# Loading a first job in one transfer, forming a decay in two parts, and placing idle transposes: a fused attention and MoE kernel

## The chip, the cores and the metric

The kernel runs on one core of one Trainium2 chip. The metric is device time in microseconds (us) of one execution. The core has a matrix engine (TensorE, PE in the profile; its weight loads are PEld), VectorE (DVE), ScalarE (ACT), GpSimd (POOL), and SyncE (SP), which here does nothing but issue DMA transfers; ScalarE can issue transfers too. Sixteen DMA engines carry the transfers of the core.

## The reference, cut to what matters

Three stages run one after the other on 4 x 576 = 2304 tokens:

```python
scores = q @ k.T / sqrt(64)                    # 4 batches x 8 heads, 576 x 576, causal
cum    = cumsum(max(s, 0))                     # one decay row of 576 per head
scores = where(causal, -1e9, scores + minimum(-(cum[q] - cum[k]), 0))
x = softmax(scores) @ v                        # -> 2304 x 512
x = (ms * relu(x @ w_in)**2 + mb) @ w_out      # 512 -> 2048 -> 512
x = maximum(x @ w1, x @ w2, x @ w3, 0) @ w_fin # 512 -> 768 -> 512
```

The weights arrive as 64-bit numbers. The result must have the accuracy of fp32, so that a product of the MoE stages is made of three matmuls on rounded parts (hi x hi, hi x lo, lo x hi), and every weight is first converted into two such parts on chip.

## The kernel before, in words

Attention is cut into jobs of one pair of heads each. The first jobs (kind A) cover the first 320 of 576 positions of a pair, the next ones (B) the rest, later ones (W) a whole pair. Query positions are taken in chunks (the first has 64 rows, the others 128); chunk `i` sees the first `W[i]` = 64, 192, 320, 448, 576 keys. For each chunk ("unit") of a job and both heads of the pair the kernel does: scores in PSUM (`qk`, L542: raw q by raw k, and L544: the decay of the chunk `dd` by a one-hot `oh` that picks the head), mask and row minimum on DVE (`least`, L563), exponential and row sum on ACT (`expo`, L569), transposes on PE (`turn_p`, L612) and a copy of them (L245 on ACT, L249 on DVE), product with v (L631). The reciprocal of the row sums (`rr`, L582) is turned (L586), split (`rt`, L594) and spread (L602), and multiplied into `x` (L639). The first MoE product (L256 to L258) begins between the jobs, and fills PE from then on.

The decay is formed once for all heads: `s` (32 heads x 576) is loaded four times, into the four groups of 32 partitions, so that both heads of a pair and both of their parts have it in place (four transfers at L342, two of them issued by ACT). L352 takes the maximum with zero, L353 makes the running sum over all 576 columns, and `difference(i)` (L358) makes the part of chunk `i` in `df`. ACT rounds `df` into `dh` (L361 for chunks 0 to 2 at once, L519 for chunks 3 and 4), and DVE makes from both the operand `dd` (L362, L523). L445 makes `dm`, a copy of the running sum that jobs of kind W load later.

A weight piece is one transfer from SP (L281) into `wg`, `stage` or `wst` and eight steps: L286 on ACT, then L289, L291, L295, L297 on DVE, a rounding (L245 on ACT or L249 on DVE), and L252 and L301 on DVE or POOL. While attention starts, these conversions are most of what DVE does.

The order on each engine is made when the program is built: a list scheduler (`Plan`) takes the steps with estimated costs, priorities, needs and buffers, and writes each engine's instructions in the order that it finds. An engine executes its list strictly in this order. `WARM` idle transposes of the identity (`warm`, L510) open PE's list. `keep` makes `KEEP` more of them in a step of lowest priority, `KEEPS` times, wherever the plan sees a hole on PE before the first MoE product; with `KEEPS` = 0 there are none. `COLD` is the planned time up to which the scheduler reckons a PE step at double cost. SP's list starts with its share of `s`, q of jobs 0 and 1 (L476, two transfers a job, one for each head), a weight piece, v, k of jobs 0 and 1 (L476), and further weight pieces.

Of the kernel before, what the change touches and what calls it, by code (L numbers as in the profile page):

```python
# [8 lines left out]
F32 = mybir.dt.float32  # L9
# [17 lines left out]
COLD = 8  # L27
DM_AT = 47.138
D_AT = -2.0
WARM = 40  # L30
KEEP = 4
KEEPS = 0
# [171 lines left out]
def fused_kernel(ctx, tc, q, k, v, s, w_in, w_out, ms, mb, w1, w2, w3, w_fin, out,  # L204
# [65 lines left out]
    def weight_steps(piece, stage_tile):  # L270
# [10 lines left out]
        nc.sync.dma_start(st.bitcast(I64), src)  # L281
# [59 lines left out]
    for g in range(4):  # L341
        (nc.sync if g < 2 else nc.scalar).dma_start(s0[g * NH:(g + 1) * NH], s.rearrange("b h s -> (b h) s"))  # L342
# [12 lines left out]
    df = atp.tile([P, OFF[-1] + W[-1]], F32, name="df", tag="p2")  # L355
    def difference(i):
# [3 lines left out]
    def split_d(a, b):  # L360
        nc.scalar.activation(dh[:, :b - a].bitcast(F32R), df[:, a:b], AF.Copy)  # L361
        nc.vector.scalar_tensor_tensor(dd[:, a:b], dh[:, :b - a], lower, df[:, a:b], op0=ALU.mult, op1=ALU.add)  # L362

    for i in range(3):
        difference(i)
    split_d(0, OFF[3])


# [316 lines left out]
    def add(key, engine, cost, prio, needs, f, *args, att=False, delay=None, **k):  # L685
# [4 lines left out]
        if engine == "SP":  # L690
            plan.add(("issue", *key), {"SP": 0.475 * cost[0] + 0.17 * (cost[0] // 3)}, prio, needs, f, *args, delay=0.65, **k)
            plan.add(key, {"DMA": cost[1] * P * 4 / 360e3}, prio, [("issue", *key)], lambda: None, delay=0.95 + (delay or 0))
            return
# [9 lines left out]
    for e, cost in (("DVE", 7.7), ("ACT", 6.8), ("Pool", 5.0)):  # L703
        add(("pre", e), e, cost, -1e9, [], lambda: None)
    add(("warm",), "PE", 0.213 * WARM / 2, -1e9, [], warm, take=[("sm", [("warm",)])])
    for i in range(3, NC):
        add(("df", i), "DVE", dve_fast(W[i]), -2.0, [("pre", "DVE")], difference, i, att=True)
        add(("dh", i), "ACT", act(W[i]), D_AT + i, [("df", i), ("dd", i - 1)], hi_d, i, att=True)
        add(("dd", i), "DVE", dve(W[i]), D_AT + i, [("dh", i)], lo_d, i, att=True)
    add(("pp",), "Pool", 1.2, 4.0, [("pre", "Pool")], rest_p, att=True)  # L710
    for x, e in enumerate(("ACT", "DVE", "DVE", "DVE")):
        add(("dm", x), e, act(S) if e == "ACT" else dve(S), DM_AT + x, [("pre", "DVE")] + [("dm", y) for y in range(x)], decays, x, att=True)
# [3 lines left out]
    for x in range(KEEPS):  # L716
        add(("keep", x), "PE", 0.109 * KEEP, 1e8, [("keep", x - 1)] if x else [("turn_p", 0, 1, 1)], keep, x, take=[] if x else [("mm", [("keep", KEEPS - 1)])])
# [3 lines left out]
    for job in jobs:  # L721
# [18 lines left out]
        if pairs:  # L740
            for key, when, m in (("q", Q_LOAD, job.q1 - job.q0), ("k", K_LOAD, job.keys)):
                add((key, n), "SP", (2, m), t0 + when, [] if key == "q" else [("q", n)], load_qk, job, key, take=[("raw", [("qk", n, u) for u in units])] if key == "q" else [], **a)
            add(("oh", n), "Pool", 0.3, t0 + TURN, [("qk", n - 2, u) for u in range(6)], one_hot, job, **a)
        else:
            for j in range(2):
                th = t0 + j * period / 2
                add(("q", n, j), "SP", (2, 2 * S), th + Q_LOAD, [], load_both, job, j, take=[("raw", [("rest", n, j, z) for z in range(PARTS)] + [("again", n, j)])], **a)
# [7 lines left out]
        for x, u in enumerate(units):  # L755
            i, k0, k1, c0, c1 = UNITS[u]
            if pairs:
# [3 lines left out]
                add(("qk", n, u), "PE", 5 * (k1 - k0) / 2400 + 0.25, at[u, 0], ready + [("dd", i) if i > 2 else ("pre", "DVE")] + [("after", z) for z in same] + order, qk, job, u,  # L761
# [65 lines left out]
    def convert(name, z, piece, stage_tile, prios, needs, ring_st, ring_a, **k):  # L827

        state = []

        def step(on=None):
            if not state:
                state.append(side_steps(piece) if name == "s" else weight_steps(piece(), stage_tile))
# [8 lines left out]
        parts = (("SP", (1, 2 * n), (), [(ring_st, back)]), ("ACT", act(n), (0,), [(ring_a, back)] if ring_a else []),  # L842
# [702 lines left out]
_INS = ['q', 'k', 'v', 's', 'moe_w_in', 'moe_w_out', 'moe_s', 'moe_b', 'moe2_w1', 'moe2_w2', 'moe2_w3', 'moe2_w_out']  # L1545
# [3 lines left out]
def _lay_out(name, a):  # L1549

    import numpy as _np
    if name in ("q", "k", "v"):
        b, h, n, d = a.shape
        if name == "v":
            a = a.reshape(b, h // 2, 2, n, d).transpose(0, 1, 3, 2, 4).reshape(b * h // 2, n, 2 * d)
        else:
            a = a.transpose(0, 1, 3, 2).reshape(b * h // 2, 2, d, n)
            a = _np.concatenate([a, a], axis=2)
# [26 lines left out]
```

## Time and profile before

| | us |
|---|---|
| median of 3 runs | 887.21 |
| lowest and highest run | 885.99, 888.48 |
| span of the profiled execution | 887.0 |
| PE busy in it | 868.2 (98%) |
| DVE busy in it | 646.5 (73%) |
| ACT busy in it | 484.7 (55%) |
| POOL busy in it | 329.1 (37%) |

The span runs from the first to the last instruction of one profiled execution. Only its span was kept, no time of its own; it lies inside the three runs' interval, 0.2 us under their median. The shares are means over the whole span: an engine with a small share can still be the one that a stage waits for, so the stretch that a change touches has to be read by itself.

### The profile page before, as it was taken

The numbers are of one execution on the slowest core, as the hardware profiler recorded it, in microseconds if no ns is written. First come the engines' busy times: TensorE is split into PE (matmuls) and PEld (weight loads), VectorE is DVE, ScalarE is ACT, GpSimd is POOL, SyncE is SP. The second block draws the span as 40 slices with busy tenths as digits, with TensorE's granted clock in tenths as the row PEclk, the third lists the DMA queues.
The fourth block names the chain that finished last, engine by engine and source line by source line (L and its number), as shares of the span: only waits on it lengthen the run. The fifth ranks groups of instructions, "written<-read, shape, count | busy, mean of one in ns | idle before, by whom it ended". The sixth has DMA issues, their size and how long they took to land.

```text
span 887.0 us, 16239 instructions
## 1 busy us (share of the span) xinstructions
PE 868.2 (98%) x5374; PEld 784.5 (88%) x5374; DVE 646.5 (73%) x1587; ACT 484.7 (55%) x1211; POOL 329.1 (37%) x361
## 2 busy tenths in 40 slices
PE   7999999999999999999999999999999999999998
PEld 6668888888888989999988888888999899989996
DVE  7999588888986888794859799744666566656650
ACT  6878999999955454453546364451225322532221
POOL 3344567566631332342324151320224322522220
PEclk9999999999999999999999999999999999999999
DMA  6654555655552466464747748449999156815501
GB/s 204 186 157 149 172 167 170 214 161 176 174 172 73 124 189 215 144 244 132 256 122 273 274 151 310 151 149 251 300 303 273 72 166 176 229 72 166 166 25 71
DMA packets 155268, 159.16 MB, mean 179 GB/s; under 512 B 10545, under 2 KB 121393, under 8 KB 155185
## 3 DMA queue, kind: packets, MB, share of 16 engines
q1 hardware_dynamic: 155088, 157.98, 57.5%
q8 instruction: 43, 0.70, 0.3%
q14 instruction: 41, 0.33, 0.1%
q10 hardware_dynamic: 96, 0.15, 0.0%
HBM read 113.72 MB, written 44.37 MB: 178 GB/s over the span
## 4 chain that ended last, share of the span: by engine, by line
PE 75%; DVE 10%; ACT 6%; DMA 5%; issue 2%; SPq 1%; POOL 0%; DVEq 0%; ACTq 0%; POOLq 0%
PE mm L256 22%; PE mm L257 22%; PE mm L258 22%; PE pt L612 3%; PE px L631 3%; PE ps L552 3%; DMA wst<-in_moe_w_out_dram 3%; ACT pp L569 2%; ACT pt L245 1%; DVE pp L563 1%; DMA x_d<-x 1%; DVE g L1037 1%; PE pr L602 1%; DMA stage<-in_moe_w_in_dram 1%; ACT set L486 1%
## 5 line engine op out<-in xcount | busy, mean ns | idle before, releaser
L252 POOL TENSOR_TENSOR gbl<-g,gbh 128x512 fp32r<-128x512 f32 (+1 forms) x50 | 64.8, 1297 | 124.5 <-ACT gbh L245 123.9
L1041 ACT ACTIVATE g<-g 128x512 f32<-128x512 f32 (+3 forms) x98 | 50.6, 516 | 79.8 <-DVE g L1037 79.1
L569 ACT ACTIVATE pp<-pp,mn 64x64 f32<-64x64 f32 (+4 forms) x160 | 88.7, 558 | 3.1 <-DVE mn L563 3.1
L252 POOL TENSOR_TENSOR set<-raw,set 64x384 fp32r<-64x384 f32 x72 | 72.8, 1036 | 38.7 <-ACT set L486 25.7
L256 PE MATMUL mm<-ty,sdp 128*128 128x384 f32 x252 | 84.2, 334 | 0.0
L257 PE MATMUL mm<-ty,sdp 128*128 128x384 f32 x252 | 84.2, 334 | 0.0
L258 PE MATMUL mm<-ty,sdp 128*128 128x384 f32 x252 | 84.2, 334 | 0.0
L612 PE MATMUL pt<-ident,pp 128*128 128x128 f32 x480 | 77.9, 278 | 3.9 <-ACT pp L569 1.6
L252 POOL TENSOR_TENSOR ga<-g,ga 128x320 fp32r<-128x320 f32 (+1 forms) x48 | 41.4, 862 | 99.1 <-ACT ga L245 98.4
L1037 DVE TENSOR_SCALAR g<-mm 128x512 f32<-128x512 f32 (+3 forms) x98 | 53.4, 545 | 31.6 <-PE mm L258 30.0
L258 PE MATMUL mm<-gbh,wb_out 128*128 128x512 f32 (+2 forms) x200 | 73.6, 368 | 0.0
L256 PE MATMUL mm<-gbh,wb_out 128*128 128x512 f32 (+2 forms) x200 | 73.6, 368 | 0.0
L257 PE MATMUL mm<-gbl,wb_out 128*128 128x512 f32 (+2 forms) x200 | 73.6, 368 | 0.0
L258 PE MATMUL mm<-xb,wb_in 128*128 128x512 f32 (+1 forms) x200 | 73.4, 367 | 0.0
L256 PE MATMUL mm<-xb,wb_in 128*128 128x512 f32 (+1 forms) x200 | 73.4, 367 | 0.0
L245 ACT ACTIVATE pt<-pt 128x256 f32<-128x256 f32 (+3 forms) x169 | 66.1, 426 | 6.9 <-PE pt L612 6.5
L563 DVE CUSTOM_DVE_ANT_0 pp<-late_keys,ps 64x64 f32<-64x64 f32 (+4 forms) x160 | 62.9, 418 | 7.3 <-PE ps L552 5.9
L612 PEld LDWEIGHTS pt<-ident,pp 128*128 128x128 f32 x480 | 55.4, 140 | 12.4 <-ACT pp L569 5.8
L257 PE MATMUL mm<-xb,wb_in 128*128 128x512 f32 (+1 forms) x170 | 61.8, 363 | 0.0
L257 PE MATMUL mm<-ga,wa_out 128*128 128x320 f32 (+2 forms) x192 | 57.2, 298 | 3.1 <-POOL ga L252 3.1
L256 PE MATMUL mm<-ga,wa_out 128*128 128x320 f32 (+2 forms) x192 | 59.8, 312 | 0.0
L256 PE MATMUL mm<-xhi,wa_in 128*128 128x320 f32 (+1 forms) x192 | 59.8, 311 | 0.0
(244 smaller groups left out, 2546.2 us busy)
## 6 DMA issues: line engine op xcount, KB each, us to landing
sdp<-s_d SPq DMA_DIRECT2D x126, 256.0 KB
s_d<-sdp SPq DMA_DIRECT2D x42, 384.0 KB
wst<-in_moe_w_dram SPq DMA_DIRECT2D x24, 384.0 KB
wst<-in_moe_w_out_dram SPq DMA_DIRECT2D x32, 256.0 KB
raw<-in_q_dram SPq DMA_DIRECT2D x24, 288.0 KB
raw<-in_k_dram SPq DMA_DIRECT2D x24, 288.0 KB
sw<-s_d SPq DMA_DIRECT2D x21, 256.0 KB
bl<-y_d SPq DMA_DIRECT2D x24, 192.0 KB
```

The source lines that it names most:

```text
L245: nc.scalar.activation(dst, src, AF.Copy, scale=1.0 if scale is None else scale)
L252: ENGINES[on].tensor_tensor(dst, a, b, op=ALU.subtract)
L256: nc.tensor.matmul(ps, lhs[0], rhs[0], start=first, stop=False)
L257: nc.tensor.matmul(ps, lhs[0], rhs[1], start=False, stop=False)
L258: nc.tensor.matmul(ps, lhs[1], rhs[0], start=False, stop=last)
L552: nc.tensor.matmul(ps[:, :k1 - k0], t[:, a, QS[i]:QS[i] + P], t[:, b, k0:k1], start=x == 0, stop=x == 1)
L563: nc.vector.tensor_tensor_reduce(out=pp[j][i][:n, k0:k1], in0=late_keys[:n, a:a + k1 - k0], in1=ps_.pop((job.n, u, j))[:n, :k1 - k0], scal ...
L569: nc.scalar.activation(p[:n, :w], p[:n, :w], AF.Exp, bias=mns[job.n, j][:n, i:i + 1], scale=-1.0, accum_out=sums[job.n % 2][:n, j, i:i + 1])
L612: nc.tensor.transpose(pt[:, c - c0, :], pp[j][i][:, c * P:(c + 1) * P], ident)
L631: nc.tensor.matmul(px_[job.n][hf][j * D:(j + 1) * D, a0 - h0:h1 - h0], vn[job.n % 2][:, c, j, :], columns(job, pr["p", job.n, j], c, c + 1 ...
L1037: nc.vector.tensor_scalar(st["g", f], st["u", f][:, :n], 0.0, None, op0=ALU.max)
L1041: nc.scalar.activation(st["g", f], st["g", f], AF.Square)
```

## The change

It has four parts.

**Decay.** `s` is loaded by one transfer of SP, whose source repeats the 32 rows four times with a stride of zero. The maximum and the running sum are made for columns 0 to 63 first and for the other 512 afterwards, and rounding and `dd` are made for each chunk apart.

**First job's q and k.** On the host q and k of a pair are stacked in one array. Job 0's part of it (128 partitions x 2 x 320) comes in one transfer, the first instruction of ACT's list. The other jobs' q and k come in one transfer (kinds A, W) or two (B) in place of four.

**Idle transposes.** `WARM` goes from 40 to 16, and `KEEPS` from 0 to 80 with one transpose in each step.

**The plan's numbers.** `COLD` goes from 8 to 5.6, and the priorities and needs of the decay's steps change, so that the scheduler writes other lists. `ON_ACT` is empty, so that what is made for it in the code is never used.

```diff
-COLD = 8
+COLD = 5.6
-D_AT = -2.0
-WARM = 40
-KEEP = 4
-KEEPS = 0
+D_0 = -50.0
+D_1 = -49.0
+D_B = 4.0
+WARM = 16
+KEEP = 1
+KEEPS = 80
...
-    for g in range(4):
-        (nc.sync if g < 2 else nc.scalar).dma_start(s0[g * NH:(g + 1) * NH], s.rearrange("b h s -> (b h) s"))
+    nc.sync.dma_start(s0, s.rearrange("b h s -> (b h) s").unsqueeze(0).to_broadcast([4, NH, S]))
+    raw_0 = atp.tile([P, 2, S], F32, name="raw", tag="raw0")
+    nc.scalar.dma_start(raw_0[:, :, :SPLIT], qk_in[0][:, :, :SPLIT])
...
-    nc.vector.tensor_scalar(s0, s0, 0.0, None, op0=ALU.max)
-    nc.vector.tensor_tensor_scan(cum, ones, s0, 0.0, op0=ALU.mult, op1=ALU.add)
+    positive(0, W[0])
+    running(0, W[0])
...
-    for i in range(3):
-        difference(i)
-    split_d(0, OFF[3])
...
-        for j in range(2):
-            nc.sync.dma_start(raw[job.n][j * D:(j + 1) * D, z, a:b], src[job.p, j, :D, a:b])
+        if (a, b) == (0, job.keys):
+            nc.sync.dma_start(t[:, :, a:b], src[:, :, a:b])
...
-        for z, src in ((0, q), (1, k)):
-            nc.sync.dma_start(t[:, z], src[job.p, j])
+        nc.sync.dma_start(t, qk_in[NP + 2 * (job.p - NP) + j])
...
+    add(("positive",), "DVE", 0.4, D_1 - 1, [("df", 0)], positive, W[0], S, att=True)
+    add(("running",), "DVE", 1.2, D_1 - 1, [("positive",), ("dd", 0)], running, W[0], S, att=True)
+    for i in range(NC):
+        z = (D_0, D_1, D_1 + 1, D_B, D_B + 1)[i]
+        add(("df", i), "DVE", dve_fast(W[i]), z - 0.5, [("running",) if i else ("pre", "DVE")], difference, i, att=True)
```

What the two programs have in a row on DVE, from the first step on `s` to the first row minimum (`s_108` holds `s`, its running sum and `dh`; `least` is shown as ISA). Before:

```order
L352 TENSOR_SCALAR s_108<-s_108 128x576
L353 SCALAR_TENSOR_TENSOR s_108<-s_108 128x576
L358 TENSOR_SCALAR df<-s_108 128x64
L358 TENSOR_SCALAR df<-s_108 128x192
L358 TENSOR_SCALAR df<-s_108 128x320
L362 SCALAR_TENSOR_TENSOR dd<-s_108,lower,df 128x576
L289 TENSOR_SCALAR wg<-wg 128x384
L358 TENSOR_SCALAR df<-s_108 128x448
L358 TENSOR_SCALAR df<-s_108 128x576
L291 SCALAR_TENSOR_TENSOR wg<-wg 128x384
L563 ISA pp_0_149,mn<-late_keys,ps 64x64
```

The same place with the change (its lines have other numbers: L359 is the maximum, L362 the running sum, L369 `difference`, L534 `dd`):

```order
L359 TENSOR_SCALAR s_108<-s_108 128x64
L362 SCALAR_TENSOR_TENSOR s_108<-s_108 128x64
L369 TENSOR_SCALAR df<-s_108 128x64
L359 TENSOR_SCALAR s_108<-s_108 128x512
L534 SCALAR_TENSOR_TENSOR dd<-s_108,lower,df 128x64
L362 SCALAR_TENSOR_TENSOR s_108<-s_108 128x512
L369 TENSOR_SCALAR df<-s_108 128x192
L369 TENSOR_SCALAR df<-s_108 128x320
L574 ISA pp_0_143,mn<-late_keys,ps 64x64
```

`dd` of the first chunk now stands behind three short steps and one long one, and the rest of the running sum behind it; `dd` of chunks 1 and 2 follows after the first row minima.

On ACT, from the rounding of chunk 3 (before, L519) or the first exponential (with the change) to the row sums of job 0 (L576). Before:

```order
L245 ACTIVATE pt<-pt 128x64 x2
L286 ACTIVATE wg<-wg 128x384
L569 ACTIVATE pp_2_151,sums_143<-pp_2_151,mn 128x320
L245 ACTIVATE pt<-pt 128x2x128 x2
L569 ACTIVATE pp_2_156,sums_143<-pp_2_156,mn 128x320
L245 ACTIVATE pt<-pt 128x3x128
L576 ACTIVATE rs<-sums_143,lower 128x2x3
L286 ACTIVATE stage<-stage 128x384
```

With the change (L289 is the first step of a conversion, L580 the exponential, L530 the rounding of `df`, L587 the row sums):

```order
L580 ACTIVATE pp_1_149,sums_137<-pp_1_149,mn 128x192
L530 ACTIVATE s_108<-df 128x448
L289 ACTIVATE stage<-stage 128x384 x2
L580 ACTIVATE pp_2_145,sums_137<-pp_2_145,mn 128x320
L289 ACTIVATE stage<-wst 128x384
L580 ACTIVATE pp_2_150,sums_137<-pp_2_150,mn 128x320
L587 ACTIVATE rs<-sums_137,lower 128x2x3
```

The first steps of three conversions, which read the transfers `stage`, `stage` and `wst`, now stand ahead of the exponentials of job 0's third unit; before, the first of them stood behind the row sums.

On PE, from the start of the list to the third unit of job 0. Before:

```order
L510 MATMUL warm<-ident 128x128 x40
L542 MATMUL ps<-raw 128x64 x2
L544 MATMUL ps<-dd,oh 128x64 x2
L542 MATMUL ps<-raw 128x192 x2
L544 MATMUL ps<-dd,oh 128x192 x2
L542 MATMUL ps<-raw 128x320 x2
```

With the change (L519 is `warm`, L525 `keep`, L553 and L555 the two parts of the scores, L623 the transposes):

```order
L519 MATMUL warm<-ident 128x128 x16
L553 MATMUL ps<-raw 128x64 x2
L555 MATMUL ps<-dd,oh 128x64 x2
L525 MATMUL warm<-ident 128x128 x14
L553 MATMUL ps<-raw 128x192 x2
L555 MATMUL ps<-dd,oh 128x192 x2
L623 MATMUL pt<-ident,pp_0_143 128x128
L623 MATMUL pt<-ident,pp_0_148 128x128
L525 MATMUL warm<-ident 128x128 x9
L553 MATMUL ps<-raw 128x320 x2
```

Fourteen idle transposes stand between the first two units and nine ahead of the third; 41 more stand between the third unit's scores and its own transposes, and the last 16 later in the two first jobs. PE's list is the same again in both programs from its 526th instruction of before on.

## Rows read from the trace of the kernel before

**Rows 1.** Busy time by stretch; columns named in the first line, clock, DMA share, GB/s
```profile
core 0: us, PE busy (x) PEld busy (x) DVE busy (x) ACT busy (x) POOL busy (x), PEclk, DMA share, GB/s
3.86:21.45 17.59, 14.51 (x100) 10.85 (x98) 15.04 (x48) 12.59 (x44) 4.00 (x16) 1.00 0.75 228
21.45:65.00 43.55, 40.30 (x284) 28.39 (x280) 43.14 (x125) 36.85 (x113) 16.03 (x19) 1.00 0.58 166
65.00:85.00 20.00, 19.48 (x146) 15.84 (x145) 18.11 (x47) 16.14 (x38) 7.74 (x8) 1.00 0.46 146
85.00:887.00 802.00, 791.80 (x4844) 727.31 (x4842) 569.41 (x1363) 417.80 (x1018) 298.44 (x304) 1.00 0.58 180
```
**Rows 2.** Waits of DVE from 3 to 25 us: us, times, longest
```profile
DVE s L352 <- DMA s<-in_s_dram: 2.0, 1, 2.0
DVE rt L594 <- ACT rt L245: 1.5, 1, 1.5
DVE dd L362 <- ACT s L361: 0.8, 1, 0.8
```
**Rows 3.** Waits of PE from 85 us to the end, the longest first
```profile
PE mm L257 <- POOL ga L252: 3.1, 4, 1.3
PE px L631 <- DVE x L639: 1.0, 1, 1.0
```
**Rows 4.** Timeline of DVE: start, us, what [idle before, releaser]
```profile
3.86 0.51 DVE L352 TENSOR_SCALAR s<-s 128x576 f32<-128x576 f32 x1 [2.01 <-DMA s<-in_s_dram]
4.41 1.36 DVE L353 TENSOR_TENSOR_SCAN s<-s 128x576 f32<-128x576 f32 x1
...
14.52 0.56 DVE L301 TENSOR_TENSOR wa_in<-wg 128x384 fp32r<-128x384 f32 x1
...
16.44 0.21 DVE L582 RECIPROCAL rr<-rs 128x12 f32<-128x12 f32 x1
...
19.84 0.28 DVE L594 TENSOR_TENSOR rt<-pr,rt 10x128 fp32r<-10x128 f32 x1 [1.49 <-ACT rt L245]
```
**Rows 5.** Chain of waits from 0 to 18 us: start, us, what
```profile
10.47 6.71 DMA stage<-in_moe_w_in_dram
...
17.20 0.57 ACT stage L286
```
**Rows 6.** Timeline of PE, its first score product
```profile
9.08 0.54 PE L542 MATMUL ps<-raw 64*128 64x64 f32 x3 [0.59 <-DMA raw<-in_k_dram]
```
**Rows 7.** DMA from 1.7 to 3.2 us, ACT's queue: packets, MB, share of 16 engines
```profile
q10 hardware_dynamic: 96, 0.15, 26.5%
```
**Rows 8.** The same columns as rows 1, two stretches of heavy transfer
```profile
1.75:2.50 0.75, 0.75 (x4) 0.75 (x5) 0.07 (x1) 0.75 (x1) 0.61 (x4) 1.00 0.91 237
9.70:13.60 3.90, 2.40 (x17) 1.50 (x16) 3.77 (x15) 3.65 (x15) 0.43 (x1) 1.00 0.98 306
```
**Rows 9.** As rows 1, while a load of four partitions (`set`, L496) runs alone
```profile
175.51:175.92 0.41, 0.41 (x6) 0.41 (x6) 0.41 (x3) 0.41 (x3) 0.41 (x2) 1.00 0.19 22
```
**Rows 10.** Durations on DVE by form, 3.7 to 12.5 us: us, mean ns, idle before
```profile
L523 DVE SCALAR_TENSOR_TENSOR dd<-s,lower,df 128x576 fp32r<-128x576 f32 x1 | 0.8, 820 | 0.1
L523 DVE SCALAR_TENSOR_TENSOR dd<-s,lower,df 128x448 fp32r<-128x448 f32 x1 | 0.7, 671 | 0.0
L358 DVE TENSOR_SCALAR df<-s 128x576 f32<-128x576 f32 x1 | 0.5, 514 | 0.0
L358 DVE TENSOR_SCALAR df<-s 128x64 f32<-128x64 f32 x1 | 0.3, 254 | 0.0
```
**Rows 11.** Weight loads of the idle transposes, 1.7 to 6 us and 6.3 to 8.3 us
```profile
L510 PEld LDWEIGHTS warm<-ident x21: 183/231/231, 1.7 to 5.9; 128*128 128x128 f32 x21
L510 PEld LDWEIGHTS warm<-ident x18: 139/140/145, 6.3 to 8.1; 128*128 128x128 f32 x18
```
**Rows 12.** Timeline of ACT: an exponential of unit 2 and the first `stage` conversion
```profile
13.96 0.55 ACT L569 ACTIVATE pp<-pp,mn 128x320 f32<-128x320 f32 x1
...
17.20 0.57 ACT L286 ACTIVATE stage<-stage 128x384 f32<-128x384 f32 x1 [0.96 <-DMA stage<-in_moe_w_in_dram]
```

More of the change, by code (lines that the diff above doesn't have):

```diff
@@ L280, in weight_steps @@
             hi, lo = hi(), lo and lo()
-        nc.sync.dma_start(st.bitcast(I64), src)
+        (queue or nc.sync).dma_start(st.bitcast(I64), src)
         yield
@@ L689, in add @@
             attention.append(key)
-        if engine == "SP":
-            plan.add(("issue", *key), {"SP": 0.475 * cost[0] + 0.17 * (cost[0] // 3)}, prio, needs, f, *args, delay=0.65, **k)
+        if engine in ("SP", "ACTQ"):
+            plan.add(("issue", *key), {"SP": 0.475 * cost[0] + 0.17 * (cost[0] // 3)} if engine == "SP" else {"ACT": 0.45 * cost[0]}, prio, needs, f, *args, delay=0.65, **k)
             plan.add(key, {"DMA": cost[1] * P * 4 / 360e3}, prio, [("issue", *key)], lambda: None, delay=0.95 + (delay or 0))
@@ L702, in fused_kernel @@
     add(("s_b",), "SP", (2, 2), 30.0, [], load_sb)
-    for e, cost in (("DVE", 7.7), ("ACT", 6.8), ("Pool", 5.0)):
+    for e, cost in (("DVE", 4.05), ("ACT", 2.5), ("Pool", 5.0)):
         add(("pre", e), e, cost, -1e9, [], lambda: None)
[L705 to L709, printed above, removed]
+    add(("warm",), "PE", 3.0, -1e9, [], warm, take=[("sm", [("warm",)])])
+    add(("positive",), "DVE", 0.4, D_1 - 1, [("df", 0)], positive, W[0], S, att=True)
[3 more added lines that the diff above has]
+        add(("df", i), "DVE", dve_fast(W[i]), z - 0.5, [("running",) if i else ("pre", "DVE")], difference, i, att=True)
+        add(("dh", i), "ACT", act(W[i]), z, [("df", i), ("pre", "ACT")] + [("dd", x) for x in ((1, 2), (3,))[i - 3]] if i > 2 else [("df", i), ("pre", "ACT")], hi_d, i, att=True)
+        add(("dd", i), "DVE", dve(W[i]), z, [("dh", i)], lo_d, i, att=True)
     add(("pp",), "Pool", 1.2, 4.0, [("pre", "Pool")], rest_p, att=True)
     for x, e in enumerate(("ACT", "DVE", "DVE", "DVE")):
-        add(("dm", x), e, act(S) if e == "ACT" else dve(S), DM_AT + x, [("pre", "DVE")] + [("dm", y) for y in range(x)], decays, x, att=True)
+        add(("dm", x), e, act(S) if e == "ACT" else dve(S), DM_AT + x, [("running",)] + [("dm", y) for y in range(x)], decays, x, att=True)
     add(("save_d",), "SP", (4, 16), DM_AT, [("dm", x) for x in range(4)], save_d, att=True)
@@ L746, in fused_kernel @@
                 th = t0 + j * period / 2
-                add(("q", n, j), "SP", (2, 2 * S), th + Q_LOAD, [], load_both, job, j, take=[("raw", [("rest", n, j, z) for z in range(PARTS)] + [("again", n, j)])], **a)
+                add(("q", n, j), "SP", (1, 2 * S), th + Q_LOAD, [], load_both, job, j, take=[("raw", [("rest", n, j, z) for z in range(PARTS)] + [("again", n, j)])], **a)
                 add(("round", n, j), "ACT", act(2 * S), th + SET_AT, [("q", n, j)] + [("set", z) for z in range(2)], round_set, job, j, take=[("hs", [("qk", n, u, j) for u in units])], **a)
@@ L760, in fused_kernel @@
                 ready = [("oh", n), ("q", n), ("k", n)]
-                add(("qk", n, u), "PE", 5 * (k1 - k0) / 2400 + 0.25, at[u, 0], ready + [("dd", i) if i > 2 else ("pre", "DVE")] + [("after", z) for z in same] + order, qk, job, u,
+                add(("qk", n, u), "PE", 5 * (k1 - k0) / 2400 + 0.25, at[u, 0], ready + [("dd", i)] + [("after", z) for z in same] + order, qk, job, u,
                     take=[("sm", [("least", n, u, j)]) for j in range(2)], **a)
@@ L1542, in fused_kernel, with _lay_out @@
         stacks[n].close()
-_INS = ['q', 'k', 'v', 's', 'moe_w_in', 'moe_w_out', 'moe_s', 'moe_b', 'moe2_w1', 'moe2_w2', 'moe2_w3', 'moe2_w_out']
+_INS = ['qk', 'v', 's', 'moe_w_in', 'moe_w_out', 'moe_s', 'moe_b', 'moe2_w1', 'moe2_w2', 'moe2_w3', 'moe2_w_out']
 _OUTS = [((2304, 512), 'float32')]
-def _lay_out(name, a):
+def _lay_out(name, inputs):
     import numpy as _np
-    if name in ("q", "k", "v"):
-        b, h, n, d = a.shape
[L1554 to L1558, printed above, removed]
+    if name == "qk":
+        b, h, n, d = inputs["q"].shape
+        a = _np.stack([inputs[x].transpose(0, 1, 3, 2) for x in "qk"], axis=3)
+        first = a[0].reshape(h // 2, 2 * d, 2, n)
+        rest = a[1:].reshape((b - 1) * h, d, 2, n)
+        a = _np.concatenate([first, _np.concatenate([rest, rest], axis=1)], axis=0)
+    else:
+        a = inputs[name]
+    if name == "v":
+        b, h, n, d = a.shape
+        a = a.reshape(b, h // 2, 2, n, d).transpose(0, 1, 3, 2, 4).reshape(b * h // 2, n, 2 * d)
     return _np.ascontiguousarray(a)
@@ L1571 @@
     for name in _INS:
-        a = _lay_out(name, inputs[name])
+        a = _lay_out(name, inputs)
         if a.dtype == _np.float64:
```

43 lines of the change are left out of this document (30 added, 13 removed).

## The prediction

> **What bounds the kernel now.** I read the busy time by stretch first [rows 1]. PE is busy 791.80 of the last 802.00 us, and the longest of the few waits it has there end on POOL and DVE, none on a transfer [rows 3]. From 85 us on PE is the bound, and its list is the same in both programs from its 526th instruction on, which is about there. So the change acts on the first 85 us, and the rest follows as a shift. Merging the later q and k transfers gives nothing by itself, since PE waits for none of them.
>
> Between 21.45 and 65 us DVE is busy 43.14 of 43.55 us and PE 40.30 [rows 1]. DVE sets the pace there: its conversions and row minima fill it, and PE follows. Before 21.45 us DVE has gaps: from its first step on `s` at 3.86 to 21.45 it is busy 15.04 of 17.59 us, so 2.55 us are idle. Its waits name most of that [rows 2]: 0.8 us in front of `dd` (it waits for ACT's rounding) and 1.5 us in front of `rt`. Ahead of 3.86 it waits 2.0 us for `s`. What the change can give is therefore what it takes from DVE's start and gaps, at most 2.55 us while `s` lands no earlier. What it can cost is a later start of DVE, a longer list, or new gaps.
>
> Why is `rt` late? The chain of waits has SP issuing one transfer after another, until `stage` at 10.47, which lands 6.71 us later, and then its conversion on ACT at 17.20 [rows 5], which stood idle for 0.96 us for it [rows 12]. The copies and the split of the reciprocals stand behind it. The reciprocal was made at 16.44 and `rt` only at 19.84 [rows 4]. The first score product waits 0.59 us for k and starts at 9.08 [rows 6].
>
> **The transfers.** The first job's q and k come as ACT's first transfer, so its four at L476 leave SP's list, and the other jobs' are fewer. That should end PE's wait for k and bring the weights some us earlier. DVE waits for no weight today (its waits have no such row [rows 2]), so the weights gain nothing directly; but an earlier `stage` can take the 1.5 us in front of `rt`.
>
> The price is in `s`. It has 128 rows of 2304 bytes, 0.295 MB. Before, four transfers of 32 rows each kept the 16 DMA engines at a share of 0.91 [rows 8]. Now it is one transfer whose source has the four copies outermost. No row shows such a load. The nearest by its outermost size is the load of four partitions into `set`: while it runs alone, the share is 0.19, which is 3 of 16 engines [rows 9]. So I bound it between 16 engines and four. A row's price is 0.1 us on its engine: ACT's half of `s` (64 rows and 32 tiny packets) took 26.5% of 16 engines in 1.5 us [rows 7], 6.36 us over 64 rows. On four engines each carries 32 rows, 3.2 us. The heavy transfer of before begins at 1.75 us; 0.295 MB at its 237 GB/s [rows 8] are through at 3.0, and DVE started at 3.86, so some 0.85 us lie behind the last packet. Alone, `s` then lets DVE start at 1.75 + 3.2 + 0.85 = 5.8. The q and k of ACT's queue share these engines: 256 rows of 1280 bytes, 16 on each engine, at 0.055 us 0.9 us in all, so up to 6.7. I take 6.2, which is 2.3 us later than now. On 16 engines `s` with q and k (0.62 MB) at 237 GB/s [rows 8] takes between 1.25 and 2.6 us, and DVE starts between 3.85 and 5.2, say 4.5.
>
> By the Trainium skill, "DMA: Bandwidth & Descriptors", "Rules for kernel authors", a leading zero-stride broadcast of c copies keeps the whole transfer on at most c engines, which speaks against this load. By that rule the start is the later one, and the share of 0.19 agrees as far as a load without a broadcast can.
>
> **The decay in two parts.** DVE gets four more instructions: the maximum and the running sum twice, and `dd` in three pieces. What an extra one costs I read from the same form at two widths [rows 10]: `df` at 64 and 576 columns takes 254 and 514 ns, so 0.22 us stand without columns; `dd` at 448 and 576 takes 671 and 820, so 0.15. With neighbours overlapping a little, 0.15 each gives 0.6 us. For the running sum there is one width only, 1.36 us [rows 4]; it is bounded by nothing and 0.3, and I count it like the others. The 0.8 us wait in front of `dd` goes, because the rounding of 64 columns on ACT is hidden behind the maximum over 512. What is late next is `dd` of chunk 1: its rounding stands behind a weight conversion and `dm` on ACT, about 0.3 us more than DVE's steps between (two `df` and two minima). Some conversion steps change engine on the way to 85 us: DVE gets three more of about 0.56 us [rows 4], and loses one of these and three copies and subtractions. I count that as nothing, within 0.5 either way.
>
> **The idle transposes.** PE makes 16 in place of 40 at the start and 80 later, 23 of them ahead of the third unit and 41 ahead of its transposes. The weight loads show the price: 231 ns up to 6 us and 140 ns after [rows 11], at the lower and the higher level of the clock (1.2 and 2.4 GHz). The 21 loads from 1.7 to 5.9 stand 0.21 us apart and the 18 from 6.3 to 8.1 0.11, and that is what one costs. PE has 3.1 us idle in the stretch up to 21.45 and DVE is the later engine. At the higher level 64 transposes are 7 us, which lie beside DVE's minima and conversions; I count nothing. If the clock stays low for a few us, because PE now stands between its 16 transposes and the first `dd`, the 14 and 9 cost 2.4 us more on PE. DVE has about that much of other work there, so up to 1 us shows.
>
> **The sum.** To the point at 21.45 us, DVE needs its start 6.2, 15.04 of work, 0.6 for the splits and 0.3 for the new gap: 22.1, if the 1.5 us in front of `rt` go. That is 0.7 later, and it is carried to the end: 887.0 + 0.7 = 887.7. The profile's span lies 0.2 under the median of the runs, so 887.9, and I say 887.8. The start of DVE (5.8 to 6.7) and the gaps (none to 1.5) make it 887.0 to 889.2.
>
> **Rivals.** *`s` on 16 engines.* For it: other loads of 128 partitions use all engines at a share of 0.98 [rows 8]. Against it: the row of 0.19. DVE then starts at 4.5, and 4.5 + 15.04 + 0.9 = 20.4, 1.0 earlier than now: 886.0 by the span, 886.2 by the median, and 885.2 to 886.6 with the bounds.
>
> *Slower: the exponentials stand behind a transfer.* ACT now converts two `stage` pieces ahead of the third unit's exponentials, which ran at 13.96 while the first of these conversions came at 17.20 [rows 12]. If the second `stage` lands later than about 15.4, where DVE would come to the reciprocal at 18 less 2 us of exponentials and 0.6 of conversion, each us of it is a us on the reciprocal. Landing as in the trace of before (17.2 for the first) would cost 2 to 3 us: 889.5 to 891. Against it: fewer issues stand ahead of it on SP, and at 306 GB/s [rows 8] the 3.2 MB up to it are there by 13.
>
> *The clock stays low.* By the Trainium skill, "TensorE: Matmul & The Clock Gate", Part 4, transposes do not count as work for the clock, so that the idle ones could not raise it. The rows differ: the loads became faster at 6.2 us with nothing but transposes done before [rows 11]. If nothing raised it here, the 64 transposes would take 13.6 us in place of 7, and after DVE's cover 1 to 3 us would show: 889 to 891.
>
> *More than the gaps.* If earlier weights also let PE fill its 3.25 idle us between 21.45 and 65, and `s` is on 16 engines, 2.5 to 3 us go: 884 to 884.7. DVE's 99% speaks against it.
>
> **How the numbers follow.** About 0.3%, 2.7 us, is what can be told from no change here: faster is under 884.5, slower over 889.9. Four engines and no new wait: 0.57, all within 0.3%. 16 engines: 0.20, of which 0.03 under 884.5. Exponentials behind the transfer: 0.12, of which 0.07 over 889.9. Low clock: 0.05, of which 0.03 over. More than the gaps: 0.06, all under. That makes faster 0.09, same 0.81, slower 0.10. The range runs from 885.2, the low end of the 16 engines, to 889.7, and leaves about 0.2 out.
>
> **What would show it.** DVE's wait for `s` is the first thing to read: a start near 6.2 proves four engines, near 4.5 sixteen. The first score product should start near 7.5. The 0.8 us wait in front of `dd` should be gone, and so should the 1.5 in front of `rt`. ACT's conversion of `stage` should not wait. The weight loads of the idle transposes show at which level they ran. If DVE is less than 98% busy between 22 and 65 us, my account by DVE is wrong. It would also be wrong if the stretch from 85 us on is not the same length to 0.3 us.

## The result and the profile after

| | before | changed |
|---|---|---|
| median, us | 886.63 (6 runs) | 893.23 (6 runs) |
| lowest and highest | 884.39, 888.48 | 891.53, 894.56 |
| span of the profiled execution | 887.0 | 891.4 |

The changed kernel is slower: the ratio is 1.0076, with a 95% interval of 1.0061 to 1.0091, 6.6 us by the medians. The prediction was 887.8 us with a range of 885.2 to 889.7, so the time lies outside it, and on the side that had a chance of 0.10.

The two profiles differ by 4.4 us only. That is an accident of the first profile: a second one of the unchanged kernel (e5, below) has a span of 884.4. A single profile of this kernel says nothing finer than some 2 us about the end; the start is another matter.

The waits of DVE from 0 to 30 us in the changed kernel (us, times, longest), to be read against [rows 2]:

```profile
DVE s L359 <- DMA s<-in_s_dram: 9.2, 1, 9.2
DVE pp L574 <- PE ps L555: 1.8, 3, 1.1
DVE one L309 <- PEq L1592: 0.8, 1, 0.8
```

DVE now waits 9.2 us for `s`, where it waited 2.0. The waits in front of `dd` and `rt` have gone, as they should, and a new one of 1.8 us for PE's scores has come. The timeline of DVE (start, us, what) places them; the rows answer to [rows 4]:

```profile
11.10 0.20 DVE L359 TENSOR_SCALAR s<-s 128x64 f32<-128x64 f32 x1 [9.25 <-DMA s<-in_s_dram]
...
12.23 0.28 DVE L534 SCALAR_TENSOR_TENSOR dd<-s,lower,df 128x64 fp32r<-128x64 f32 x1
...
17.39 0.35 DVE L574 CUSTOM_DVE_ANT_0 pp<-late_keys,ps 128x192 f32<-128x192 f32 x1 [1.06 <-PE ps L555]
...
28.11 0.28 DVE L605 TENSOR_TENSOR rt<-pr,rt 10x128 fp32r<-10x128 f32 x1
```

DVE starts at 11.10 us in place of 3.86, 7.24 later. The busy times by stretch (columns as in [rows 1]) show that little gives that back:

```profile
3.86:21.45 17.59, 10.97 (x66) 9.26 (x65) 8.71 (x30) 7.38 (x22) 2.61 (x16) 1.00 0.73 189
21.45:65.00 43.55, 41.29 (x323) 30.62 (x322) 41.91 (x128) 35.97 (x119) 10.47 (x14) 1.00 0.54 159
65.00:85.00 20.00, 20.00 (x142) 16.04 (x141) 18.86 (x50) 17.83 (x43) 5.94 (x7) 1.00 0.45 148
```

Up to 21.45 us DVE did 8.71 us of work in place of 15.04. Afterwards it is busy 96% of the time up to 65 us (41.91 of 43.55 us), so it can hardly catch up, and from 65 to 85 us PE has no idle time at all.

Why `s` came so late is in the DMA's stretches (the same columns; the last two are the share of the 16 engines that is busy, and GB/s):

```profile
6.00:8.00 2.00, 0.04 (x2) 0.00 (x0) 0.00 (x0) 0.00 (x0) 0.18 (x3) 1.00 1.06 209
8.00:10.00 2.00, 0.00 (x0) 0.00 (x0) 0.00 (x0) 0.00 (x0) 0.00 (x0) 1.00 1.11 181
10.00:12.00 2.00, 0.00 (x0) 0.00 (x0) 0.83 (x4) 0.06 (x1) 0.00 (x0) 1.00 0.95 294
```

All engines show as busy from 6 to 10 us, with q, k, v and weights of the next steps, and yet move 181 to 209 GB/s; from 10 to 12 us, in which `s` comes through, it is 294. The same stretches of e1 (below), which differs only in how `s` lies in memory, move 361 and 365 GB/s at the same shares:

```profile
6.00:8.00 2.00, 2.00 (x20) 1.79 (x20) 1.96 (x7) 0.38 (x1) 1.39 (x5) 1.00 1.05 361
8.00:10.00 2.00, 0.88 (x7) 0.41 (x5) 1.04 (x5) 2.00 (x9) 0.00 (x0) 1.00 1.07 365
```

SP's queue felt it as well. Its last v load here had to wait until `s` had landed (the first row, a wait of SP), and the weight pieces `stage` behind it went out at 11.65 us, later than the 10.47 of before [rows 5]:

```profile
SPq L513 <- DMA s<-in_s_dram: 5.5, 1, 5.5
```

```profile
5.09 0.43 SPq L511 DMA_DIRECT2D vn<-in_v_dram  x1
11.09 0.49 SPq L513 DMA_DIRECT2D vn<-in_v_dram  x1
11.65 1.33 SPq L284 DMA_DIRECT2D stage<-in_moe_w_in_dram  x2
```

### The profile page after: what moved, and what is told of

It reads as the page before. It is cut to its first block, busy times and chain, and to the rows that moved or that the text cites. A ratio compares the mean times of both kernels' runs of the same rounds, so it can differ in the third digit from the quotient of the medians.

```text
span 891.4 us, 16272 instructions
## 1 busy us (share of the span) xinstructions
PE 873.1 (98%) x5430; PEld 790.5 (89%) x5430; DVE 640.9 (72%) x1590; ACT 486.8 (55%) x1215; POOL 324.5 (36%) x360
## 4 chain that ended last, share of the span: by engine, by line
PE 85%; DVE 5%; DMA 4%; ACT 4%; issue 1%; POOL 0%; SPq 0%; DVEq 0%; ACTq 0%; POOLq 0%
PE mm L259 23%; PE mm L260 23%; PE mm L261 23%; PE pt L623 5%; PE px L642 4%; PE ps L563 3%; PE ps L553 1%; ACT pp L580 1%; PE warm L525 1%; DMA s<-in_s_dram 1%; ACT pt L248 1%; PE pr L613 1%; DMA wst<-in_moe_w_out_dram 1%; DMA x_d<-x 1%; DMA raw<-in_qk_dram 1%
## 5 line engine op out<-in xcount | busy, mean ns | idle before, releaser
L580 ACT ACTIVATE pp<-pp,mn 64x64 f32<-64x64 f32 (+4 forms) x160 | 88.7, 558 | 3.5 <-DVE mn L574 3.5
L623 PE MATMUL pt<-ident,pp 128*128 128x128 f32 x480 | 78.8, 278 | 1.6 <-ACT pp L580 1.0
L248 ACT ACTIVATE pt<-pt 128x64 f32<-128x64 f32 (+3 forms) x171 | 67.8, 427 | 9.5 <-PE pt L623 8.5
L623 PEld LDWEIGHTS pt<-ident,pp 128*128 128x128 f32 x480 | 55.7, 141 | 9.6 <-ACT pp L580 4.6
```

What stands on the lines that cost most here:

```text
L248: nc.scalar.activation(dst, src, AF.Copy, scale=1.0 if scale is None else scale)
L580: nc.scalar.activation(p[:n, :w], p[:n, :w], AF.Exp, bias=mns[job.n, j][:n, i:i + 1], scale=-1.0, accum_out=sums[job.n % 2][:n, j, i:i + 1])
L623: nc.tensor.transpose(pt[:, c - c0, :], pp[j][i][:, c * P:(c + 1) * P], ident)
```

## The experiments

The theory after the result: the source with four copies outermost holds the load of `s` on four of the 16 DMA engines, where it also has to share them. The rival: the load spreads, and `s` is late because q, k and the weights are in front of it.

### Is it the shape of the load? (e1, e2, e3)

e1 has `s` four times in memory, so that the same transfer reads 128 rows:

```diff
-    nc.sync.dma_start(s0, s.rearrange("b h s -> (b h) s").unsqueeze(0).to_broadcast([4, NH, S]))
+    nc.sync.dma_start(s0, s.rearrange("g b h s -> (g b h) s"))
```

> The changed kernel, but `s` lies four times in memory, so that its one transfer reads 128 rows without a stride of zero. Theory 1 (the source with four copies outermost holds the transfer on four of the 16 DMA engines): with 128 rows it spreads, DVE's first step on `s` starts at 4 to 5.2 us in place of 11.10, and the 6 to 7 us go with it: 886 to 887.5. Theory 2 (`s` is late because q, k and the weights are in front of it on the engines, however many it uses): it still starts after 8 us and the time stays at 891 to 893.

e2 has the four loads of before (SP and ACT two each) in the changed kernel:

```diff
-    nc.sync.dma_start(s0, s.rearrange("b h s -> (b h) s").unsqueeze(0).to_broadcast([4, NH, S]))
+    for g in range(4):
+        (nc.sync if g < 2 else nc.scalar).dma_start(s0[g * NH:(g + 1) * NH], s.rearrange("b h s -> (b h) s"))
```

> The changed kernel, with `s` in four transfers of 32 rows as before, two of them ahead of q and k on ACT's queue. Theory 1: each spreads over 16 engines; DVE starts at 4 to 5 us; the time is that of e1 within 1 us, and q and k of the first job come up to 1 us later, which nobody sees. Theory 2: two of the four are ahead of q and k, so DVE still starts after 6 us, behind the rest.

e3 is the reverse, the kernel before with that one line of the change.

> The kernel before, with its four loads of `s` replaced by the one of SP with the repeated source, and nothing else. Theory 1: the load alone makes DVE start at 8 to 11 us (it shares its four engines with q, k and weights), and the time is 4 to 7 us above before: 891 to 894. Theory 2: nothing is in front of it here (q and k come behind it on the same queue), so DVE starts at 4 to 5 us and the time is before's within 1 us.

Measured, as ratios to the kernel before: e1 1.0026 (1.0013 to 1.0040), e2 1.0028 (1.0014 to 1.0042), e3 1.0067 (1.0045 to 1.0089). The first steps of DVE on `s`, of e1 and of e3:

```profile
3.65 0.31 DVE L359 TENSOR_SCALAR s<-s 128x64 f32<-128x64 f32 x1 [1.80 <-DMA s<-in_s_dram]
```

```profile
9.10 0.46 DVE L351 TENSOR_SCALAR s<-s 128x576 f32<-128x576 f32 x1 [7.25 <-DMA s<-in_s_dram]
```

With the same queue, the same place in it and the same bytes landed, e1 starts at 3.65 us, a little earlier than before's 3.86 and 7.45 us earlier than the changed kernel. The rival falls: in e3 nothing is in front of `s`, and it still starts at 9.10. The load alone makes the kernel before 0.67% slower, about as much as the whole change. (In e3 the load of k waited for `s` too, 3.4 us on SP's queue; the first scores still waited for `dd` and not for k, 0.75 us.) e1 missed its expected time by 2 us, however: with `s` in time the rest of the change still costs 0.26%.

### How many engines, and what does the load cost by itself? (e4, e12, e15)

e4 was to hold all other transfers behind `s`:

> The changed kernel, with every other transfer held back until `s` has landed (SP first writes one element of it to memory and so waits; q and k of the first job follow on SP). It measures the load of `s` with the engines to itself. Theory 1: 32 rows of 0.093 us on each of four engines are 3.0 us; with the first packet at 1.8 to 3.4 us and about 1 us behind the last, DVE starts at 5.8 to 7.5 us, and a quarter of the engines is busy meanwhile. Theory 2: 16 engines, DVE at 3.9 or earlier. The time is later than the changed kernel's or near it, since the first q and k now come after `s`.

It did not measure that. The holding transfer was put behind q and k of the first two jobs in SP's list, so that these still shared the engines; `s` was in at 9.06 us, when SP's wait ended. (The whole kernel took 896.36 us in its one run.) e12 places it in the first planned step of SP:

```diff
         if job.n == 0:
             raw[0] = raw_0
+            nc.sync.dma_start(first_d, s0[:1, :1])
+            nc.sync.dma_start(raw_0[:, :, :SPLIT], qk_in[0][:, :, :SPLIT])
             plan.slot("raw")
```

> The changed kernel with all transfers of SP and ACT held behind the load of `s` (SP writes one element of it to memory first, and so waits until `s` has landed; this time q and k of jobs 0 and 1 are behind it too). If four engines at 0.1 us for each of 32 rows were the right price, `s` lands at 5.8 us (the wait of SP ends there). If the first packet comes late or rows take longer even alone, it lands at 7 or later. The rest of the load's 11 us would then be the sharing with q, k and the weights.

SP's row in e12, and the stretches while `s` alone was under way:

```profile
7.45 0.27 SPq L476 DMA_DIRECT2D first_d<-s  x1
```

```profile
2.00:3.00 1.00, 1.00 (x6) 1.00 (x6) 0.00 (x0) 0.02 (x1) 0.75 (x4) 1.00 0.20 35
3.00:4.00 1.00, 1.00 (x7) 1.00 (x6) 0.00 (x0) 0.00 (x0) 0.85 (x5) 1.00 0.32 48
4.00:5.00 1.00, 1.00 (x6) 1.00 (x5) 0.00 (x0) 0.00 (x0) 1.00 (x9) 1.00 0.19 71
5.00:6.00 1.00, 0.42 (x2) 0.01 (x1) 0.00 (x0) 0.00 (x0) 1.00 (x5) 1.00 0.26 99
6.00:7.00 1.00, 0.00 (x0) 0.00 (x0) 0.00 (x0) 0.00 (x0) 0.21 (x3) 1.00 0.11 41
```

With nothing else on the engines, DVE starts at 7.23 us. The share is about a quarter, four of 16, on the average from 2 to 6 us (0.19 to 0.32); 99 GB/s is the rate while the rows follow each other. The packets of the load say the same (e12 from 1 to 7.2 us):

```profile
DMA packets 132, 0.29 MB, mean 48 GB/s; under 512 B 4, under 2 KB 4, under 8 KB 132
```

Beside its 128 rows it has four tiny packets, where two of the loads of before had 32 [rows 7], 16 each. That fits one tiny packet for each engine that a transfer uses.

The rate is the price of a row that I took (4 engines x 2304 bytes in 0.1 us are 92 GB/s). What I had not counted is that the load moves only 35 to 71 GB/s before 5 us. So 7.2 us in place of my 5.8 is the load alone, and from 7.2 to 11.1 is the sharing, 3.9 us where I had at most 0.9. e4 divides it: with q and k of two jobs beside it `s` was in at 9.06 us, some 1.8 us later than alone, and the other 2 us belong to the changed kernel, where ACT's queue brings q and k of the first job and v and weights follow on SP's.

e15 splits the load in two transfers of SP with two copies each:

```diff
-    nc.sync.dma_start(s0, s.rearrange("b h s -> (b h) s").unsqueeze(0).to_broadcast([4, NH, S]))
+    for g in range(2):
+        nc.sync.dma_start(s0[2 * g * NH:(2 * g + 2) * NH], s.rearrange("b h s -> (b h) s").unsqueeze(0).to_broadcast([2, NH, S]))
```

> The changed kernel with `s` in two transfers of SP, each with a source of two copies. If the number of copies outermost sets the number of engines, each transfer runs on two, and if these are the same two, 64 rows stand on each: at 0.1 us a row alone 6.4 us, with the neighbours' share more: DVE starts at 12 us or later, and the time is 894 or more. If the engines of the two differ, DVE starts at about 11 as in the changed kernel. If the copies don't matter, earlier than 11.

```profile
13.66 0.20 DVE L360 TENSOR_SCALAR s<-s 128x64 f32<-128x64 f32 x1 [11.81 <-DMA s<-in_s_dram]
```

It starts at 13.66 us and takes 899.53 us (one run). Fewer copies in a transfer make it later, so their number counts. The last stretch of its load, when the other transfers are through, shows on how many engines it runs:

```profile
12.00:13.00 1.00, 0.00 (x0) 0.00 (x0) 0.00 (x0) 0.00 (x0) 0.00 (x0) 1.00 0.13 48
```

The share is 0.13, two of 16, and the rate half of e12's 99 GB/s. By the Trainium skill, "DMA: Bandwidth & Descriptors", "Rules for kernel authors", a leading zero-stride broadcast of c copies keeps the transfer on at most c engines; e12's share of a quarter and e15's of 0.13 agree with it.

### Where the other 2.3 us are (e6, e7, e9, e10)

e6 is e1 without the idle transposes (the loop in `keep` runs zero times); all other instructions keep their order.

> e1 (the changed kernel with `s` stacked in memory) without the 80 idle transposes, every other instruction in the same order. Theory 'transposes hidden': DVE's row minima no longer stand behind 14 and 9 transposes, PE loses up to 8.7 us of work that nothing waited for, and the time is e1's within 0.7 us (889.3); if the clock falls without them, PE at the lower level costs 1 to 4 us more. Theory 'transposes in the way': 1 us or more faster than e1.

e7 is the kernel before with only the q and k part of the change. The plan is told nothing, so the order is that of before:

```diff
+    raw_0 = atp.tile([P, 2, S], F32, name="raw", tag="raw0")
+    nc.scalar.dma_start(raw_0[:, :, :SPLIT], qk_in[0][:, :, :SPLIT])
...
-        for j in range(2):
-            nc.sync.dma_start(raw[job.n][j * D:(j + 1) * D, z, a:b], src[job.p, j, :D, a:b])
+        if (a, b) == (0, job.keys):
+            nc.sync.dma_start(t[:, :, a:b], src[:, :, a:b])
```

> The kernel before with the q and k part alone: stacked arrays, the first job as a transfer of ACT's queue (behind ACT's two loads of `s`), later jobs in one transfer or two, and the order of all other instructions as before. Theory 'DVE is the bound': the first scores wait for `dd` in place of k (0.3 us earlier at most), `stage` comes some us earlier and the 1.5 us wait in front of `rt` goes: 1 to 1.8 us faster than before. Theory 'something else takes its place': within 0.5 us of before.

e9 adds the decay in two parts, written out by hand, again in the order of before:

```diff
+    positive(0, W[0])
+    running(0, W[0])
+    difference(0)
+    round_d(0, OFF[1])
+    positive(W[0], S)
+    rest_d(0, OFF[1])
+    running(W[0], S)
```

> e7 with the decay in two parts by hand (64 columns, then 512), `s` still in four loads, and the order of all other instructions as before: the changed kernel's ideas without its plan and its idle transposes. If the split helps, DVE's wait in front of `dd` goes and the first scores start near 7 us: 0.5 to 1 us under e7. If it only adds instructions, it is 0.3 to 0.6 us over e7. Against e1 it tells what the new plan and the idle transposes cost: e1 minus this one.

e10 adds to e9 39 idle transposes of PE in the holes of the first job, through a helper called behind its scores and transposes:

```diff
+        if job.n == 0:
+            idle((0, 9, 6)[u] if u < 3 else 0)
```

> e9 (the kernel before with q, k and decay changed by hand, in the order of before) with 39 idle transposes of PE in the waits of job 0. In e9 the granted clock was at the lower level from 12.1 to 22.3 us, and DVE waited 1.2 us for PE's scores there. If that wait matters, the clock stays up, the 1.2 us go, and the time is 0.5 to 1.2 us under e9 (885.7 to 886.4). If it is covered, the time is e9's within 0.4 us.

| | ratio to before | 95% interval |
|---|---|---|
| e1, the change with `s` in time | 1.0026 | 1.0013 to 1.0040 |
| e6, e1 without idle transposes | 1.0030 | 1.0019 to 1.0040 |
| e7, q and k alone | 0.9990 | 0.9979 to 1.0001 |
| e9, q, k and decay | 0.9992 | 0.9979 to 1.0004 |
| e10, e9 with idle transposes | 0.9998 | 0.9979 to 1.0016 |

The idle transposes bring nothing and cost nothing that shows in the time. They do seem to hold the clock up: from 3.6 to 21.45 us the granted clock is 1.00 in the profiles of e1 and e10, which have them, and 0.66, 0.90 and 0.74 in those of e6, e7 and e9, which don't. It is not them alone, since the kernel before, without them, has 1.00 in its first profile and 0.81 in its second (e5). These are one stretch of e6, the same of e1, and one of e9; in e6 and e9 PE is at the lower level (0.50 of full) throughout:

```profile
9.40:23.00 13.60, 9.87 (x41) 6.21 (x43) 12.32 (x41) 11.93 (x40) 0.29 (x1) 0.50 0.52 156
```

```profile
9.40:23.00 13.60, 13.50 (x114) 11.08 (x115) 13.29 (x46) 12.49 (x43) 0.74 (x2) 1.00 0.58 180
```

```profile
12.10:22.30 10.20, 8.99 (x44) 6.39 (x46) 7.95 (x28) 8.26 (x33) 0.00 (x0) 0.50 0.39 116
```

Ten us and more at half the clock, and e9 is level with e7 and e6 within 0.4 us of e1. That is not because nobody waits for PE: in its stretch e6's DVE does 12.32 us of work in place of e1's 13.29, and waits 1.2 us for PE's scores. A loss of 1 us is within the intervals, so whether it is made good later or only hidden in the noise is open.

The ideas of the change (q and k early, decay in two parts, transposes in the holes) come to 0.9990 to 0.9998 when the order of before is kept. e1, which has the same ideas in the order that the plan makes with its new numbers, is at 1.0026, and e2, whose four loads of `s` are those of e9 and e10, at 1.0028. So the new plan costs some 2 to 3 us, and the ideas gain 1 us at most. By the plan I mean all that still differs: the order, the engines that some conversion steps run on, `dd` of chunks 1 and 2 made apart, and 16 transposes at the start in place of 40. These were not taken apart; e10's interval overlaps those of e1 and e2, e9's does not.

### Which part of the new order? (e8, e11, e13)

The trace of e1 shows two new waits. One is in front of `dd` of chunk 1, which stands on ACT behind a weight conversion and `dm`. The other is far behind the change, at 247 us: the plan now converts weight piece 15 ahead of piece 14 there, and DVE stands behind a conversion on ACT whose data come later. DVE's rows in e1:

```profile
9.03 0.42 DVE L534 SCALAR_TENSOR_TENSOR dd<-s,lower,df 128x192 fp32r<-128x192 f32 x1 [0.96 <-ACT s L530]
...
247.20 0.29 DVE L292 TENSOR_SCALAR wb<-wb 128x256 int32<-128x256 int32 x1 [1.50 <-ACT wb L289]
```

e8 emits the rounding of chunk 1 ahead on ACT, e11 puts the steps at 247 us back, e13 does both. All hold single steps of the finished plan back:

```diff
+            if key == ("dm", 0) or engine == "ACT" and key[0] == "w" and ("dh", 1) not in seen:
+                held.append(f)
+                continue
```

```diff
+        until = {("w", "s", 15, 1): ("w", "s", 14, 4), ("w", "s", 15, 2): ("w", "s", 14, 6), ("w", "s", 15, 3): ("w", "s", 14, 7), ("w", "s", 15, 4): ("w", "s", 14, 7),
+                 ("w", "s", 15, 5): ("w", "s", 14, 8), ("w", "s", 15, 7): ("relua", 1, 1, 0), ("x_hi", 15, 1): ("squarea", 1, 1, 5), ("w", "s", 17, 4): ("hia", 1, 1, 5)}
```

> e1 with the rounding of chunk 1 ahead of the weight conversion and of `dm` on ACT, so that DVE does not wait for it; all other instructions in the same order. Theory 'that wait costs': the 0.96 us in front of `dd` of chunk 1 goes and the time with it, 0.7 to 1 us under e1 (888.4). Theory 'lost later anyway': no difference within 0.4 us, because the plan's other order behind 21 us sets the end.

> e1 with eight steps of DVE and ACT at about 246 us (conversion of two weight pieces) put back in the order of before; all else as in e1. In e1 the first step of piece 15 stands ahead of piece 14's on ACT, DVE waits 1.5 us for it, and PE 1.1. If the plan's later order is the loss, the time is 0.8 to 1.2 us under e1 (888.3), and PE has no wait for DVE there. If not, as e1 within 0.4 us.

> e1 with both reorderings, of e8 (rounding of chunk 1 ahead on ACT) and of e11 (the steps at 246 us in the order of before). If the 2.3 us that e1 is over before come from these two places, it is 1.2 to 1.8 us under e1 and within 0.8 us of before (ratio 1.000 to 1.001). If they come from the plan's other changes before 93 us, it stays at 1.0015 or more.

Measured: e8 1.0017 (1.0004 to 1.0031), e11 1.0018 (0.9996 to 1.0039), e13 1.0015 (1.0002 to 1.0029). Each is under e1's 1.0026, though not by more than the intervals, and both together gain no more than either alone. In e8 the wait in front of `dd` of chunk 1 is gone, and 0.57 us came in front of `dd` of chunk 2. The wait at 247 us is gone in e11.

But that wait does not come from the order alone. The changed kernel and e8 have the same lists there as e1, and the changed kernel's profile has 0.3 us of the wait and e8's none; neither has PE's 1.1 us (e2's has 0.5). In e1 the transfer of piece 15 came late in that one execution: its conversion on ACT waited 2.35 us for it, and in e8 0.63. PE's list shows better where time is lost. I take the same instruction in each profile, counted back from the list's end, and compare with e5, a second profile of the kernel before (next section):

| PE later than in e5, us | at 116 us of e5 | at 301 us |
|---|---|---|
| e1 | 0.9 | 2.2 |
| e2 | 2.2 | 2.9 |
| e6 | 2.4 | 3.0 |
| e8 | 3.3 | 3.3 |
| e11 | 2.4 | 2.6 |
| e13 | 2.3 | 2.4 |
| e7, e9, e10 | -0.3, 0.5, 1.1 | -0.5, 0.5, 1.1 |

These are single profiles, but all with the new plan except e1 have lost 2.2 us or more before 116 us, and those with the order of before 1.1 at most. So the plan's cost seems to lie at the start, and neither wait of e1 explains it: the second is mostly e1's own, and without the first e8 is no earlier.

In e13 it is PE's wait at 49 us that is longer than elsewhere (e1 has 1.1 us at this place). It waits for an exponential there, before the clock's level falls for 3.4 us from 50.2 on:

```profile
48.93 0.55 PE L623 MATMUL pt<-ident,pp 128*128 128x128 f32 x3 [1.95 <-ACT pp L580]
```

So the two places are a part of it at best, and 1.3 us of e13 (0.15%) stay with the plan's other changes at the start. Which of these it is was not settled.

### Chance, and the q and k part once more (e5, e14)

e5 is the kernel before, unchanged, profiled again.

> The kernel before, profiled a second time. Its first profile has 3.1 us of PE's waits for POOL at 315 to 358 us (four waits on `ga`), where the profiles of the changed kernels have 0.6 to 1.6. Theory 'chance': a second profile has 0.6 to 1.6 as well and a span 1 to 2 us under 887.0, so that spans of single profiles can't be compared to better than 2 us. Theory 'the change removes it': again 3 us.

Its span is 884.4 us, and of the 3.1 us that PE waited for POOL at 315 to 358 us in the first profile [rows 3] nothing is left. They were chance, of one execution. That is why the shift of 8 us, which PE's list still has at 300 us between the two profiles, is 4.8 at the end: the changed kernel's profile has 0.6 us of these waits. Against the second profile PE's list is 7.25 us late at 116 us and 7.40 at the end, and DVE's first step on `s` starts 7.40 us later (11.10 against 3.70). From 116 us on the rest is a shift there, to 0.15 us.

e14 is e7 once more, with more rounds.

> e7 once more with more rounds, as the candidate that beats both: the kernel before with the q and k part alone and the order of before. Expected again at 0.999 of before (0.9 us faster), now with an interval that excludes 1; if its gain was chance, the ratio is within 0.0004 of 1.

The ratio is 0.9994 (0.9983 to 1.0005). Two measurements of e7 lie at 0.9990 and 0.9994, both intervals touching 1. It beats the changed kernel; that it beats the kernel before is likely and not shown.

## Why the prediction was wrong, point by point

**The step that failed is the term of `s`.** I had the right mechanism (four engines, chance 0.57) and took 6.2 us for DVE's start, between 5.8 and 6.7. It is 11.10. The miss has two halves. Alone, I began the rows at 1.75 us as the old transfers did, and e12 shows little moving before 4 to 5 us: 7.2 in place of 5.8. Sharing, I counted q and k of the first job, 0.9 us, but SP went on issuing q, k, v and weights behind `s`, and with them it is 3.9 us. That they stood on the four engines of `s` is argued from the rows of 6 to 10 us (181 to 209 GB/s at a share above 1); that they made it late is shown by e12 and e4. The upper bound had no row under it for a transfer that is slow while its queue goes on, and I took the price of the quiet case for it.

**A second term was wrong too, and that the corrected sum fits is in part luck.** Put into the sum, 4.9 us more make 892.7, against the measured 893.2. But with `s` in time the same sum fails: e1's start at 3.65, 2.55 before my 6.2, makes 885.3, and e1's ratio is about 889.5 on that scale, 4 us more. From e1 to the changed kernel DVE starts 7.45 us later and the time grows by only 4.4 (1.0026 to 1.0076). So 3 us of the later start don't reach the end, and the plan's new lists, which I counted as nothing, within 0.5 us either way, cost 2 to 3 us when `s` is in time (e1 and e2 against e9 and e10). That a late `s` hides this cost is the likely reading and not shown; where the plan loses it was not settled.

**My own sign against the account by DVE came.** I wrote that it is wrong if DVE is less than 98% busy between 22 and 65 us. It is 96%, with waits of 0.5 us for ACT's row sums and 0.3 for PE among the rest, and from 65 to 85 us PE is never idle. DVE sets the pace less strictly there than I said.

**The sums.** Two of the ranges are added up short: 889.2 should be 889.5 by its own bounds, and for 16 engines 886.6 should be 886.9. Neither is near the measured time.

**The 16 engines** (chance 0.20) did not come. e1 shows what that would have been: DVE at 3.65, earlier than my 4.5, and still a time 2.3 us over before. That rival was therefore mispriced too, by some 3 us: its sum lacked the plan's cost as well.

**"The rest follows as a shift"** held in the changed kernel, from 116 us on. The place was not quite right: by the records of the two traces PE's lists become the same at 99 us of before, at its 638th instruction, and not at its 526th (84 us), and DVE's and ACT's at about 94. These two differ again from 244 to 257 us, which I had not seen. The changed kernel lost nothing there; e1 lost 1.1 us of PE, in one profile.

**The waits that go.** The 0.8 us in front of `dd` went and so did the 1.5 in front of `rt`. The second did not go for my reason, an earlier `stage`: `stage` went out later than before (11.65 us against 10.47), and DVE came to `rt` only at 28.11. With `s` in time (e1), 0.96 us came in front of `dd` of chunk 1 (I had 0.3), because the weight conversion ahead of it on ACT waited for its transfer.

**The clock.** PE stood between its 16 transposes and the first `dd`, and the level stayed low as I had said it could: 14 transposes take 3.25 us at 13 us and nine take 1.26 us at 18 in the changed kernel, 0.23 and 0.14 each. The weight loads of the 14 take 226 ns, as those at the lower level in [rows 11]; the column of the granted clock reads 1.00 there, as it does in the first us of before [rows 8], so it does not show this stretch. DVE waited 1.8 us for PE's scores; I had up to 1.

```profile
L525 PEld LDWEIGHTS warm<-ident x14: 183/226/229, 13.0 to 15.6; 128*128 128x128 f32 x14
```

```profile
13.01 3.25 PE L525 MATMUL warm<-ident 128*128 128x128 f32 x14
...
17.78 1.26 PE L525 MATMUL warm<-ident 128*128 128x128 f32 x9
```

**The exponentials behind a transfer** (chance 0.12) did not happen. The two conversions of `stage` ran at 19.15 us without a wait of ACT, and the transfers were there. With the late `s` that was no test of it, but in e1 they ran at 12.58 us without a wait as well.

**Merged transfers** gain nothing by themselves, I wrote. e7 and e14 measure q and k together at 0.4 to 0.9 us under before, which is no contradiction and no proof.

## What to carry to other kernels

A load that is repeated over partitions by a stride of zero saves issues and pays with engines: read its outermost size as the number of DMA engines it may use, and lay the copies out in memory or keep several loads. Price such a load under the traffic that its own queue sends behind it, not alone; the two differed here by 3.9 us. When a plan orders the instructions, compare every engine's list to its end before saying that the rest is a shift, and test an idea in the old order first, so that its gain isn't mixed with that of a new order. When a corrected sum meets the measured time, try it on a second run before believing its other terms, and before a wait is taken for the cost of an order, see whether other profiles with the same order have it.

## What the runs showed of the hardware that I had not expected

A load on four engines is late even alone: 35 and 48 GB/s from 2 to 4 us, 71 and 99 from 4 to 6 (e12). While it runs under traffic, the engines show as busy (shares of 1.06 and 1.11) and move 181 to 209 GB/s, where the kernel with `s` stacked in memory moves 361 to 365 at shares of 1.05 and 1.07 (e1). And half the clock for ten us and more (e6, e9) cost less here than the runs can tell, though DVE waited for PE's scores in it.
